# A new written-out order of operations, and the last output tile in two column halves, in a fused attention and FFN kernel

## The chip, the cores and the metric

The kernel runs on 1 core of one Trainium2 chip. The metric is the device time of one execution in microseconds (us). The time before is 236.06, the median of 3 runs (235.92 to 236.71).

## The reference, cut to what matters

```python
# q, k, v: (B=8, H=8, S=576, D=64); pool = 8, so Sp = 72 pooled keys
k_p = k.reshape(B, H, Sp, 8, D).mean(axis=3)
v_p = v.reshape(B, H, Sp, 8, D).mean(axis=3)
attn = softmax(q @ k_p.T / sqrt(D))            # 576 x 72 a head
x = (attn @ v_p), heads side by side            # (B, 576, 512)
h = relu(x @ w_in)                              # (B, 576, 1024)
conv = sum over 3 taps of conv_w[tap] * h shifted by tap - 1 along the sequence
out = (h * sigmoid(conv)) @ w_out               # (B, 576, 512), float32
```

## The kernel before, in words

Eight sequences are worked on in four groups of two. A group has nine tiles of up to 128 rows: tiles 0 to 3 hold rows of its first sequence, tile 4 holds 64 rows of both, tiles 5 to 8 hold rows of the second one.

**Loads.** Every input comes through the DMA queue that POOL (GpSimd) issues to: k, q and v of each sequence, w_in in two halves, w_out. They turn float32 into bf16 on the way. POOL also builds the pool matrix (L299, affine selects), the head mask (L320) and the identity. Buffers are reused: one for raw k, four for q, three for v, so later loads wait until an earlier user is done.

**Attention of a tile.** K is pooled by TensorE (PE) with the pool matrix for sequences 0 and 1 (`prep_k`, L374 and L384), and on DVE for the others (`pool_pair` L406, then a turn by PE, L412). V is pooled on DVE (`prep_v`, L434, L438, with the widened head mask of L337). q is turned by PE (`prep_q`, L464 in the form of 18 matmuls a half, L468 in the form of 36) and copied out of PSUM (L474). Then come scores (PE, L503 or L516), the maximum (DVE, L529), the shift (PE L549 in group 0, DVE L541 later), exp (ACT, L567), the turn of the exponentials (PE and a copy in groups 0 and 1, a DMA transpose on the SP queue in groups 2 and 3), values (PE, L603), the division (DVE, L616 and L618), and the turn of the result into xT (PE and a copy, or a DMA transpose).

**FFN of a sequence.** `ffn_in` (L648; for sequence 0 tile by tile, L669, in both kernels) multiplies by w_in into PSUM, ACT applies relu (L657, L679), `ffn_conv` (L730) does the convolution as matmuls with diagonal 64x64 matrices, ACT takes tanh (L741), DVE gates (L752, L755, L759), `ffn_out` (L764) multiplies by w_out, DVE or ACT copies the tile out of PSUM (L775), and SP stores it (L787), as two DMAs of 64 rows.

**What sets the order.** The program is made as a graph of some 970 operations (`add`). `Graph.order` (L138) then emits them in the sequence that the table `ORDER` gives: entry n stands for operation n // 2, its last bit chooses between the engines that it may run on, and -1 is a fill matmul, a product of zeros that occupies PE. Each engine works through its own instructions in that sequence. `FORMS` chooses between two ways of writing `prep_k`, `prep_q` and the scores. `PLACES` gives the PSUM banks, of which there are 8. The SBUF buffers of a ring (rings such as `osb`, `tg`, `e`, `x`) are taken in turn.

**The last tile** (group 3, tile 8) is accumulated in one PSUM bank by 8 matmuls of 512 columns. Its left 256 columns are copied by DVE, its right 256 by ACT; when both are done, SP stores the first 64 rows and ACT's queue the other 64 (L1098).

Of the kernel before, what the change touches and what calls it, by code (L numbers as in the profile page):

```python
# [33 lines left out]
class Graph:  # L34
# [75 lines left out]
    )  # L110
    FORMS = (
        0, 0, 1, 1, 0, 1, 1, 1, 0, 0, 0, 0, 0, 1, 1, 0, 1, 0, 0, 0, 0, 0, 0, 0, 0, 1, 0, 0, 0, 1, 0, 1, 0, 1, 1, 1, 1, 1, 1, 1,
        0, 0, 0, 0, 0, 0, 0, 0, 1, 0, 1, 0,
    )
    PLACES = (
# [8 lines left out]
    )  # L124

# [34 lines left out]
def kernel(  # L160
# [38 lines left out]
    def bank(token):  # L199
        return psum[:, token.slots[0], :]  # L200
# [956 lines left out]
```

## Time and profile before

| what | us |
|---|---|
| median of 3 runs | 236.06 (235.92 to 236.71) |
| the profiled execution | 237.85 |
| its span, first to last instruction | 235.6 |
| mean granted TensorE clock | 0.981 |
| DVE busy / ACT busy / POOL busy | 173.9 / 146.3 / 28.0 |
| first real matmul (K of sequence 0) | 6.98 |
| PE without a stop from | 151.83 |

In the profile PE is matmuls, PEld weight loads, DVE VectorE, ACT ScalarE, POOL GpSimd, SP SyncE; L764 is line 764 of the kernel before, as printed above. An x with a number counts instructions, and `<-` names what ended a wait. PEclk is the granted share of TensorE's clock. Matmuls overlap each other in the records, so a busy PE is not PE at its peak: the pace of a group is read from where it follows itself without a gap, as in the chain of work, in which 4 matmuls of 512 columns take 0.86 us and 4 of 288 columns 0.49.

### The profile page before, as it was taken

To read this page: it belongs to the slowest core of one execution; us is meant where nothing else is said; L and a number is where in the kernel's file an instruction comes from. 1 tells how busy PE (TensorE), PEld (TensorE's weight loads), DVE (VectorE), ACT (ScalarE), POOL (GpSimd) and SP (SyncE) were. 2 spreads that over 40 slices of the span, in tenths; PEclk is the share of its full clock that TensorE was granted. 3 is DMA by queue.
4 is the path that set the end of the run, shared out by engine and by line. 5 is a ranking of instruction groups with operands and counts; after the bars stand their busy time and mean duration, and the time that the engine had idled before them with its cause. 6 is when DMAs were issued, how large, how long until landed. Compare 5 with 4: busy or idle time off the path is not lost. (4 is left out here: it accounts for less than half of the span.)

```text
span 235.6 us, 7790 instructions
## 1 busy us (share of the span) xinstructions
PE 216.2 (92%) x3362; PEld 150.8 (64%) x3362; DVE 173.9 (74%) x365; ACT 146.3 (62%) x246; POOL 28.0 (12%) x45
## 2 busy tenths in 40 slices
PE   6697899969999899988998899899999999999991
PEld 2455799756678777556764477568766665875440
DVE  4489886996999999988799779769757625716510
ACT  2245668896888997749766576358434563685320
POOL 7930731110000520300000000000000000000000
PEclk9979999997999999999999999999999999999998
DMA  5999999999940299999135777656665642601596
GB/s 88 163 186 207 207 207 207 207 207 206 191 98 3 19 199 185 230 179 171 25 70 32 155 150 137 130 124 132 91 133 116 130 85 46 136 3 38 112 203 143
DMA packets 44006, 31.51 MB, mean 134 GB/s; under 512 B 23596, under 2 KB 39364, under 8 KB 43972
## 3 DMA queue, kind: packets, MB, share of 16 engines
q0 software_dynamic: 16288, 16.26, 42.9%
q1 hardware_dynamic: 27604, 14.64, 32.3%
q8 instruction: 26, 0.43, 0.8%
q10 hardware_dynamic: 80, 0.13, 0.1%
q14 instruction: 8, 0.07, 0.1%
HBM read 32.52 MB, written 9.44 MB: 178 GB/s over the span
## 5 line engine op out<-in xcount | busy, mean ns | idle before, releaser
L764 PE MATMUL psum<-w_out_sb,gT 128*128 128x512 bf16 x288 | 70.2, 382 | 0.0
L648 PE MATMUL psum<-xT,w_in_sb 128*128 128x288 bf16 x448 | 63.7, 286 | 2.3 <-ACT tg L741 2.3
L648 PEld LDWEIGHTS <-w_in_sb 128*128 128x128 bf16 x448 | 42.0, 98 | 16.5 <-issue 2.8
L657 ACT ACTIVATE hT<-psum 128x576 bf16<-128x576 f32 x56 | 35.0, 649 | 23.8 <-PE psum L648 23.6
L741 ACT ACTIVATE tg<-psum 128x576 bf16<-128x576 f32 x64 | 37.5, 652 | 12.5 <-PE psum L730 11.0
L764 PEld LDWEIGHTS <-gT 128*128 128x128 bf16 x288 | 27.0, 98 | 25.4 <-issue 0.7
L529 DVE TENSOR_REDUCE negm<-psum 128x8 f32<-128x576 f32 (+1 forms) x36 | 27.1, 752 | 5.8 <-PE psum L516 3.9
L730 PE MATMUL psum<-hT,dw 64*64 64x288 bf16 (+4 forms) x1152 | 30.3, 246 | 1.1 <-ACT eT L592 0.3
L730 PEld LDWEIGHTS <-dw 64*64 64x64 bf16 x1152 | 25.3, 107 | 8.0 <-issue 7.3
L618 DVE TENSOR_TENSOR x<-psum,r 128x512 bf16<-128x512 f32 x36 | 24.9, 692 | 1.2
L775 ACT COPY osb<-psum 128x512 f32<-128x512 f32 (+1 forms) x26 | 14.6, 581 | 16.9 <-PE psum L764 15.1
L759 DVE TENSOR_TENSOR gT<-gT,hT 128x1152 bf16<-128x1152 bf16 x32 | 24.3, 758 | 1.1
L567 ACT ACTIVATE e<-sd 128x576 bf16<-128x576 f32 x27 | 18.2, 684 | 7.9 <-DVE sd L541 4.9
L775 DVE COPY osb<-psum 128x512 f32<-128x512 f32 (+1 forms) x11 | 7.3, 667 | 19.9 <-PE psum L764 14.5
L541 DVE TENSOR_TENSOR sd<-psum,negm 128x576 f32<-128x576 f32 x27 | 20.4, 755 | 0.8
L755 DVE TENSOR_SCALAR gT<-tg 64x576 bf16<-64x576 bf16 x64 | 19.7, 309 | 1.5 <-ACT tg L741 0.2
L603 PE MATMUL psum<-vm,eT 128*128 128x130 bf16 (+5 forms) x240 | 18.4, 222 | 1.4 <-DVE negm L529 1.4
L752 DVE TENSOR_SCALAR gT<-tg 128x576 bf16<-128x576 bf16 x32 | 9.5, 305 | 11.7 <-ACT tg L741 11.6
L603 PEld LDWEIGHTS <-eT 128*128 128x128 bf16 (+1 forms) x240 | 14.5, 100 | 4.3 <-DMA eT<-e 1.5
L434 DVE TENSOR_TENSOR v<-v 128x1280 bf16<-128x1280 bf16 (+2 forms) x24 | 13.0, 542 | 0.2
L592 ACT COPY eT<-psum 128x640 bf16<-128x640 bf16 x15 | 10.3, 691 | 4.4 <-PE psum L578 4.1
L616 DVE RECIPROCAL r<-psum 128x8 f32<-128x8 f32 x36 | 7.3, 202 | 7.8 <-PE psum L603 7.6
(73 smaller groups left out, 205.9 us busy)
## 6 DMA issues: line engine op xcount, KB each, us to landing
out_dram<-osb SPq DMA_DIRECT2D x71, 128.0 KB, 2.4
v<-in_v_dram POOLq DMA_DIRECT2D x8, 512.0 KB, 18.5
qp<-in_q_dram POOLq DMA_DIRECT2D x7, 576.0 KB, 14.0
kk<-in_k_dram POOLq DMA_DIRECT2D x3, 1152.0 KB, 13.9
w_in_sb<-in_moe_w_in_dram POOLq DMA_DIRECT2D x2, 512.0 KB, 17.0
w_out_sb<-in_moe_w_out_dram POOLq DMA_DIRECT2D x1, 1024.0 KB, 20.0
kk<-in_k_dram POOLq DMA_DIRECT2D x2, 288.0 KB, 4.5
kk<-in_k_dram POOLq DMA_DIRECT2D x1, 576.0 KB, 12.8
```

The costliest lines, as they stand in the source:

```text
L529: nc.vector.tensor_reduce(out=a["m"][0:rows], in_=a["s"][0:rows, :, 0:2 * KW].rearrange("p a (h s) -> p a h s", s=Sp), axis=AX.X, op=OP.ma ...
L541: nc.vector.tensor_tensor(out=a["d"][0:rows], in0=a["s"][0:rows, :, 0:2 * KW].rearrange("p a (h s) -> p a h s", s=Sp), in1=a["m"][0:rows]. ...
L603: nc.tensor.matmul(out=a["o"][lo:hi, h // 4, (h % 4) * (D + 1):(h % 4 + x1 - x0) * (D + 1)], lhsT=a["eT"][:, j, lo:hi], rhs=buf("vm", b)[: ...
L618: nc.vector.tensor_tensor(out=a["x"][0:rows].rearrange("p (a h d) -> p a h d", a=2, d=D), in0=ov[:, :, :, 0:D], in1=r[0:rows].unsqueeze(3) ...
L648: nc.tensor.matmul(out=banks(ps)[:, j, 0:SC], lhsT=w_in_block(dc, fb), rhs=buf("xT", g)[:, dc, i * S + j * SC:i * S + (j + 1) * SC], start ...
L657: nc.scalar.activation(out=buf("hT", b)[:, fb, :].rearrange("p (a s) -> p a s", a=2), in_=banks(ps)[:, :, 0:SC], func=ACT.Relu, scale=0.5,)
L730: nc.tensor.matmul(out=banks(pss[r ^ c])[c * D:(c + 1) * D, j, lo:hi], lhsT=dw[r * D:(r + 1) * D, tap * n_fb + fb, :], rhs=hT[r * D:(r + 1 ...
L741: nc.scalar.activation(out=tg.rearrange("p (a s) -> p a s", a=2), in_=banks(ps)[:, :, 0:SC], func=ACT.Tanh, scale=0.5,)
L755: nc.vector.tensor_scalar(out=gate[r * D:(r + 1) * D, fb], in0=tg[(1 - r) * D:(2 - r) * D], scalar1=1.0, scalar2=None, op0=OP.add)
L759: nc.vector.tensor_tensor(out=gate[:, both], in0=gate[:, both], in1=buf("hT", b)[:, both], op=OP.mult)
L764: nc.tensor.matmul(out=bank(ps)[0:rows, :], lhsT=buf("gT", g)[:, fb, t * P:t * P + rows], rhs=w_out_sb[:, fb, :], start=(fb == 0), stop=(f ...
L775: copy(out=osb[0:rows, columns], in_=bank(ps)[0:rows, columns])
```

## The change

The three tables are replaced. The new `ORDER` has 21 fill matmuls where there were 25. By the engines that it chooses, ACT makes 29 output copies and DVE 8 (26 and 11 before, the last tile's halves counted each), DVE makes 4 copies of turned exponentials (3) and 2 of K of sequence 0 (1). By the new `FORMS`, 12 turns of q take the form of 18 matmuls and 6 that of 36 (9 and 9 before, without sequence 0's first ones, which are shorter); of the scores of the 36 tiles 23 take the form of 4 matmuls, 2 that of 8, and 11 that of 16 (26, 1 and 9). `PLACES` now gives the buffer of every ring, so SBUF buffers are no longer taken in turn.

At the start, POOL issued or did before: k 0 (two parts), identity, pool matrix, q 0 (two parts), q 1, v 0, k 1, head mask, q 2, w_in (two halves), v 1, k of group 1, q 3, w_out, q 4. Now: k 0 (two parts), first part of q 0, head mask, second part of q 0, pool matrix, identity, v 0, q 1, k 1, q 2, w_in (two halves), v 1, q 3, k of group 1, q 4, w_out. On PE, 17 fills, K of sequence 0, q's first part and the turn of the convolution weights become 11 fills, the turn of the convolution weights, K, q's first part, 5 fills. On DVE, the clearing of the v and kT buffers and the widened mask stand ahead of the copies of K.

The last tile is made in two column halves: 8 matmuls of 256 columns for each, each in a PSUM bank of its own, each copied by one engine and stored by two DMAs of 64 rows and 256 columns. The matmuls of tile 6 of the group stand partly between the halves. All the rest of the graph is the same; some planned durations in it, which the written-out order doesn't read, change too.

```diff
-    ORDER = (18, 4, 2, 0, 26, 8, 10, 16, 12, 30, -1, -1, -1, ...)
+    ORDER = (18, 24, 4, 6, 2, 8, 10, -1, 14, -1, 36, -1, 28, ...)
...
             for k in o.uses:
-                if k.slots is None and k.ring == "ps":
+                if k.slots is None:
                     i = next(places)
                     k.slots = list(range(i, i + k.n))
-                elif k.slots is None:
-                    i = taken[k.ring] = taken.get(k.ring, -1) + 1
-                    k.slots = [i % self.rings[k.ring]]
...
+    def half_columns(x):
+        return slice(x * d_model // 2, (x + 1) * d_model // 2)
+
-    def ffn_out(g, t, j, ps):
+    def ffn_out(g, t, fbs, ps, columns=slice(0, d_model)):
         rows = rows_of(g, t)
-        for fb in range(n_fb // 2 * j, n_fb // 2 * (j + 1)):
+        for fb in fbs:
             nc.tensor.matmul(
-                out=bank(ps)[0:rows, :],
+                out=bank(ps)[0:rows, columns],
                 lhsT=buf("gT", g)[:, fb, t * P:t * P + rows],
-                rhs=w_out_sb[:, fb, :],
+                rhs=w_out_sb[:, fb, columns],
...
-    def ffn_store(g, t, queue, only=None):
+    def ffn_store(g, t, queue, only=None, columns=slice(0, d_model)):
...
-                    out=out[b].rearrange("(p c) d -> c p d", c=C)[c],
-                    in_=osb[j * TB:(j + 1) * TB, :],
+                    out=out[b].rearrange("(p c) d -> c p d", c=C)[c, :, columns],
+                    in_=osb[j * TB:(j + 1) * TB, columns],
...
+            if b == B - 1 and n == len(n_outs[b]) - 1:
+                o = None
+                for x in range(2):
+                    sm = token("ps")
+                    o = add(pe(*[P * 2] * 8), key + x, lambda t=t, x=x, sm=sm: ffn_out(g, t, range(n_fb), sm, half_columns(x)),
+                            after=need + [wout, o], uses=[sm, gtok[g]], mode=FULL, count=16)
+                    c = add(either(0.42, 0.38), key + x, None, after=[o], uses=[osb, sm])
+                    c.emit = lambda c=c, t=t, x=x, sm=sm: ffn_copy(g, t, sm, copier(c), half_columns(x))
+                    for r, (e, queue) in enumerate((("SP", nc.sync), ("ACT" if x else "SP", nc.scalar if x else nc.sync))):
+                        add({e: 0.59}, key + x, lambda t=t, x=x, r=r, queue=queue: ffn_store(g, t, queue, r, half_columns(x)),
+                            after=[c], uses=[osb], land=(2.0, 0, 1))
+                continue
...
-            if b == B - 1 and n == len(n_outs[b]) - 1:
-                o = [add(d, key, lambda t=t, sm=sm, x=x, copy=copy: ffn_copy(g, t, sm, copy, slice(x * P * 2, (x + 1) * P * 2)),
-                         after=[o], uses=[osb, sm])
-                     for x, (d, copy) in enumerate(((dve(0.4), nc.vector.tensor_copy), (act(0.4), nc.scalar.copy)))]
-                for x, (e, queue) in enumerate((("SP", nc.sync), ("ACT", nc.scalar))):
-                    add({e: 0.59}, key, lambda t=t, x=x, queue=queue: ffn_store(g, t, queue, x), after=o, uses=[osb], land=(2.0, 0, 1))
-                continue
```

More of the change, by code (lines that the diff above doesn't have):

```diff
@@ L59 @@
     ORDER = (
[50 rows of a table removed]
[50 rows of a table added]
     )
     FORMS = (
-        0, 0, 1, 1, 0, 1, 1, 1, 0, 0, 0, 0, 0, 1, 1, 0, 1, 0, 0, 0, 0, 0, 0, 0, 0, 1, 0, 0, 0, 1, 0, 1, 0, 1, 1, 1, 1, 1, 1, 1,
-        0, 0, 0, 0, 0, 0, 0, 0, 1, 0, 1, 0,
+        1, 1, 1, 0, 0, 0, 1, 1, 0, 0, 0, 0, 0, 0, 0, 0, 0, 0, 0, 0, 0, 0, 0, 0, 0, 1, 0, 0, 0, 1, 0, 1, 0, 1, 1, 1, 1, 0, 1, 1,
+        1, 0, 0, 0, 0, 0, 0, 1, 0, 1, 1, 1,
     )
     PLACES = (
[8 rows of a table removed]
[18 rows of a table added]
     )
@@ L138, in order @@
     def order(self):
-        forms, places, spares, taken, done, seen = iter(self.FORMS), iter(self.PLACES), list(self.spares), {}, [], set()
+        forms, places, spares, done, seen = iter(self.FORMS), iter(self.PLACES), list(self.spares), [], set()
         for n in self.ORDER:
@@ L819 @@
     START = -2 * SLOTS
-    LATE = 2.0
+    LATE = 1.8
     RATE, RATE_FIRST = 400e3, 285e3
@@ L867 @@
         graph.spares.append(Op({"PE": 0.216}, 0, lambda t=t: fill(t), [t], FULL, None, 2))
-    c1 = add({"DVE": 0.6}, soon(), clear_pool_matrix)
+    c1 = add({"DVE": 1.5}, soon(), clear_pool_matrix)
     p0 = add({"POOL": 1.6}, first("pm"), build_pool_matrix, after=[c1])
@@ L874 @@
     cwtok = token("ps")
-    cwp = add({"PE": 0.1}, soon(), lambda: turn_conv_weights(cwtok), after=[idf, cwl], uses=[cwtok])
-    zv = add({"DVE": 0.55}, soon(), lambda: clear(*[v0[TB:P, 4, :] for v0 in buffers["v"]]))
+    cwp = add({"PE": 0.1}, soon(), lambda: turn_conv_weights(cwtok), after=[idf, cwl], uses=[cwtok], count=2)
+    zv = add({"DVE": 0.84}, soon(), lambda: clear(*[v0[TB:P, 4, :] for v0 in buffers["v"]]))
     ze = add({"DVE": 0.25}, soon(), lambda: clear(*[e[:, 4 * KW:] for e in buffers["e"]]))
-    zk = add({"DVE": 0.8}, soon(), lambda: clear(*buffers["kT"][1:]))
+    zk = add({"DVE": 1.25}, soon(), lambda: clear(*buffers["kT"][1:]))
     p1 = add({"DVE": 0.35}, soon(), double_pool_matrix, after=[p0])
@@ L884 @@
     hmw = add(dve(1.15), soon(), widen_mask, after=[hm])
-    dw0 = add({"DVE": 0.2}, soon(), lambda: build_conv_matrices(0, cwtok), after=[cwp], uses=[cwtok])
+    dw0 = add({"DVE": 0.3}, soon(), lambda: build_conv_matrices(0, cwtok), after=[cwp], uses=[cwtok])
     dwo = [add({"DVE": 1.0}, START + Graph.DW + n, lambda n=n: build_conv_matrices(n), after=[dw0]) for n in (1, 2)]
@@ L891, in add_load_pair @@
         loads["kk", g] = add({"POOL": 0.65}, key, lambda: load_pair(g), uses=[kk[g]], land=(LATE, 2 * kb, RATE))
-    picked = add({"DVE": 0.5}, START + Graph.DW - 1, build_pick, after=[c0])
+    picked = add({"DVE": 0.95}, START + Graph.DW - 1, build_pick, after=[c0])
     for b in (1, 2, 3):
@@ L1015, in add_att @@
         if turn_by_dma(g, t):
-            o = add({"SP": 1.29}, key, lambda: att_send(g, t), after=[o, ze], uses=[e, eT], land=(1.7, 0, 1))
+            o = add({"SP": 1.29}, key, lambda: att_send(g, t), after=[o, ze], uses=[e, eT], land=(2.1, 0, 1))
         else:
@@ L1027, in add_att @@
         if b0 >= Graph.X_DMA:
-            o = add({"SP": 1.29}, key, lambda: att_out(g, t), after=[o], uses=[x, xtok[g]], land=(1.7, 0, 1))
+            o = add({"SP": 1.29}, key, lambda: att_out(g, t), after=[o], uses=[x, xtok[g]], land=(2.1, 0, 1))
         else:
@@ L1071, in add_ffn @@
             conv = add({"PE": 0.75}, w + 6 * f2 + Graph.QCONV + nudge("c", 4 * b + f2), lambda f2=f2, cbs=cbs: ffn_conv(b, f2, cbs),
-                       after=relu[fbs[0]] + relu[fbs[1]] + dwo, uses=cbs + tgs + [htok[b], gtok[g]], mode=QUARTER, count=64 + 12 * i)
+                       after=relu[fbs[0]] + relu[fbs[1]] + dwo, uses=cbs + tgs + [htok[b], gtok[g]], mode=QUARTER, count=64 + 16 * i)
             for fb, cb, tg in zip(fbs, cbs, tgs):
@@ L1086, in add_out @@
             key += nudge("ot", 9 * g + t)
-            sm, osb = token("ps"), token("osb", g, t)
+            osb = token("osb", g, t)
+            need = [a for x in groups[g][0:i + 1] for a in gdone[x]]
+            if b == B - 1 and n == len(n_outs[b]) - 1:
[10 more added lines that the diff above has]
+                continue
+            sm = token("ps")
             o = None
             for j in range(2):
-                need = [a for x in groups[g][0:i + 1] for a in gdone[x]]
-                o = add(pe(*[512] * 4), key, lambda t=t, j=j, sm=sm: ffn_out(g, t, j, sm), after=need + [wout, o],
+                o = add(pe(*[512] * 4), key, lambda t=t, j=j, sm=sm: ffn_out(g, t, range(4 * j, 4 * j + 4), sm), after=need + [wout, o],
                         uses=[sm, gtok[g]], mode=FULL if rows == P else HALF, count=8)
-            if b == B - 1 and n == len(n_outs[b]) - 1:
-                o = [add(d, key, lambda t=t, sm=sm, x=x, copy=copy: ffn_copy(g, t, sm, copy, slice(x * P * 2, (x + 1) * P * 2)),
-                         after=[o], uses=[osb, sm])
-                     for x, (d, copy) in enumerate(((dve(0.4), nc.vector.tensor_copy), (act(0.4), nc.scalar.copy)))]
-                for x, (e, queue) in enumerate((("SP", nc.sync), ("ACT", nc.scalar))):
-                    add({e: 0.59}, key, lambda t=t, x=x, queue=queue: ffn_store(g, t, queue, x), after=o, uses=[osb], land=(2.0, 0, 1))
-                continue
             o = add(either(0.69, 0.585), key, None, after=[o], uses=[osb, sm])
```

126 rows, old and new, of tables (ORDER, PLACES) are left out of this document.

## The prediction

> **What bounds the kernel now.** First the page: busy time, the 40 slices.
>
> ```profile
> PE 216.2 (92%) x3362; PEld 150.8 (64%) x3362; DVE 173.9 (74%) x365; ACT 146.3 (62%) x246; POOL 28.0 (12%) x45
> ...
> PEclk9979999997999999999999999999999999999998
> DMA  5999999999940299999135777656665642601596
> ```
>
> PE's 92% is a mean over unlike stages, its clock dips twice, and the DMA engines are full only up to about 64 us. So the second view is the table by stretches (us; then busy PE, PEld, DVE, ACT, POOL; granted clock, DMA share, GB/s), cut where the stages change.
>
> ```profile
> 6.98:24.00 17.02, 13.22 (x304) 9.15 (x304) 13.47 (x33) 8.04 (x16) 6.66 (x12) 0.90 1.22 193
> 24.00:52.40 28.40, 25.05 (x564) 21.59 (x563) 24.21 (x53) 21.54 (x35) 9.16 (x12) 1.00 1.23 207
> 52.40:64.00 11.60, 11.60 (x108) 7.83 (x103) 9.18 (x15) 8.91 (x14) 0.00 (x0) 0.85 1.23 205
> 64.00:122.00 58.00, 54.97 (x1020) 41.76 (x1017) 54.31 (x112) 46.43 (x81) 6.46 (x9) 1.00 0.72 117
> 122.00:151.90 29.90, 27.36 (x383) 17.91 (x382) 25.21 (x45) 18.14 (x30) 0.00 (x0) 1.00 0.69 123
> 151.90:230.90 79.00, 78.87 (x984) 50.65 (x983) 44.73 (x98) 41.33 (x71) 0.00 (x0) 1.00 0.51 105
> ```
>
> From 151.9 on PE never stops, so a reordering there gains nothing but the tail. From 64 to 122 PE and DVE are both near full (54.97 and 54.31 of 58): each makes the other wait. Up to 64 the loads run at 207 GB/s without a break, and PE and DVE both have holes. Third, the chain that ended last. It is nothing but PE from 151.83, then two copies one after the other:
>
> ```profile
> 151.83 0.04 issue
> ...
> 216.91 13.93 PE psum L764 x64
> ...
> 230.92 0.44 DVE osb L775
> ...
> 231.38 0.37 ACT osb L775
> ```
>
> Fourth, the timeline of the start and the landings of single loads:
>
> ```profile
> 6.98 1.32 PE L374 MATMUL psum<-pm,kk 128*64 128x144 bf16 x36
> 18.98 1.70 DVE L434 TENSOR_TENSOR v<-v 128x1280 bf16<-128x1280 bf16 x3
> 21.43 0.87 PE L603 MATMUL psum<-vm,eT 128*128 128x130 bf16 x12
> 29.74 1.05 PE L669 MATMUL psum<-xT,w_in_sb 128*128 128x128 bf16 x16
> ```
> ```profile
> v<-in_v_dram POOLq DMA_DIRECT2D x1, 64.0 KB, 10.6
> ```
> ```profile
> w_in_sb<-in_moe_w_in_dram POOLq DMA_DIRECT2D x1, 512.0 KB, 17.9
> ```
>
> The last part of V of sequence 0 is issued at 7.95 and lands 10.6 us later, at 18.6; DVE pools it at 18.98, and the first values matmul runs at 21.43. The second half of w_in is issued at 11.52 and lands at 29.4; the first matmuls that need it run at 29.74. Both are waits for data.
>
> **The sum is made against** the profiled execution: 237.85 us, of which the span is 235.6 and 2.25 lie around it. The median of the runs is 236.06, 1.79 lower; I take the difference found on the span off that median. A measurement here tells about 0.3% (0.7 us) from no change.
>
> **Start, POOL and PE.** In the new order POOL issues from 1.31: K 1.55 (to 2.86), first part of q 0.77 (3.63), head mask 0.79 (4.42), second part of q 0.75 (5.17), pool-matrix selects 1.63 (6.80), identity 0.6 (7.4), then V. PE's first real work is now the turn of the convolution weights, behind ACT's copy of the identity (0.30, to 7.75); with its 0.3 the K matmuls start at 8.1, where they started at 6.98: **1.1 late**. q is no longer late (it was issued at 4.98 and landed 4.4 later, at 9.4; now issued at 2.86, behind K in the same queue). K 1.2, q 0.5, five fill matmuls 1.1: first scores near 11.1 against 10.34, 0.8 late.
>
> **Start, DVE.** Between the first maximum (11.13) and the values at 21.43 DVE had clearing of kT 1.22, half the convolution matrices 0.89, mask_wide 1.14 and a q copy 0.75 on top of the maxima. The new order clears kT and builds mask_wide ahead of or beside the K matmuls, where DVE waited, and sets the others later. What is left there: four maxima 3.0, q copy 0.5, mask columns 0.5, V 1.70 and 0.66: 6.4 from 11.45, so 17.8, where 21.4 was: **3.5 early**, if V is there. V is issued at about 7.4, as before, but ahead of q of sequence 1 (576 KB, 2.8 us at 207 GB/s): it lands near 15 instead of 18.6.
>
> **Start, loads.** That lead can't all be kept: the FFN of sequence 0 needs w_in, behind the same bytes as before (K, q, V of 0; K, q of 1; q of 2). What moves it is the hole in the stream: after K landed at 6.9 the first 256 KB of q, worth 1.3 us at 207 GB/s, landed at 9.4, so 1.1 was idle. V took 4.5 us for 2.8 us worth of bytes, another 1.7 that may or may not go. w_in lands 1.1 to 2.8 earlier; I take **2.0**, the middle, since PE is busy 9.8 of 10 us from 30 to 40 and carries such a lead on unchanged.
>
> **44 to 64.** PE loses most here: 0.40 busy in 50 to 52, with a 1.8 us wait put down to issue, and then the clock at 0.61 and 0.53 from 52 to 56. I added, for each order, the row durations of all that stands ahead of one and the same operation. Ahead of the turn of the pooled K of group 1 stand 39.2 us of DVE work before and 37.3 after; q of sequences 3 and 4 also moves up. DVE is full there (9.7 of 10), so that is up to 1.9; I take half, **1.0**, as the work is deferred and not gone.
>
> **64 to 152.** The same sums: at the last convolution of sequence 2, PE 96.5 and DVE 111.1 before, 100.2 and 115.0 after: DVE leads by 14.6 and 14.8. At the last of sequence 4: 11.4 and 12.3. In between it is worse: at the last values of group 1, 9.9 (t 100.6) and 12.1. A larger lead of DVE work means that PE waits longer: 0.2 to 2.2 lost, nearest to the two later points, **0.4**.
>
> **Forms and fills.** Four fills fewer (0.22 each, -0.9); three q turns take the 18-matmul form (0.63) for the 36-matmul form (0.33): +0.9. Scores change form within 0.1. Copies: DVE has three output copies fewer (0.69 each) and two others more (0.48, 0.31), ACT the reverse: inside the DVE sums above. Nothing net.
>
> **Tail.** The last tile was 8 matmuls of 512 columns, then DVE 0.44 and ACT 0.37 in series (one bank), then a store on SP and one on ACT at 231.78, landing 2.3 and 2.6 later. Now 16 matmuls of 256 columns: the same columns, 8 more starts, which no row here shows; bounds from the nearest rows: 0 (w_in matmuls of 288 columns follow at 0.12 each, without a gap for weights) to 8 x 0.1 (a weight load, mean 98 ns, if none were hidden); I take 0. The second half has its own bank, one copy of 0.42, saving 0.4. But on SP its store stands behind four others: two of the first half, two of tile 6, whose copy ends 0.2 before PE does; they take 0.6 each, so the last store is issued 1.15 after PE's end, where it was 0.9. ACT's lands earlier, SP's at 1.15 + 2.3 = 3.45 after PE's end; it was 3.5. **0.1 gained**, with bounds of -0.5 and +0.8.
>
> **Sum:** -2.0 - 1.0 + 0.4 - 0.1 = -2.7: span 232.9, profiled 235.15, median **233.3**.
>
> **A rule and the rows.** The clock fell to half for about 3.4 us twice: 0.83 over 10 to 20 and over 50 to 60, after stretches in which PE was at work about half the time (0.90 of 2 in 8 to 10, 0.40 of 2 in 50 to 52), with no single wait over 1.9. The Trainium skill (TensorE: Matmul & The Clock Gate, Part 1) has the clock halve after an idle window of about 3.4 us. By that rule neither dip should be here; the trace disagrees, so short waits count, and the new start, with PE idle from about 5.9 to 7.75, can dip too.
>
> **Rivals.** (1) *More is gained:* the q and K work of the next sequences moves up, so the 1.8 us wait and the dip at 52 (3.4 us at half speed, 1.7) go altogether, with w_in 2.8 early: -2.8 - 1.8 - 1.7 = -6.3, 229.8. For it: w_out and q of sequence 4 stand early enough in the new queue. Against: the wait is put down to issue, not to data. (2) *Given back:* the lead is spent where DVE is full, 64 to 122; the 2.2 at group 1 is not recovered, so 3.0 - 2.2 - 0.1: 235.2 to 236. (3) *Slower:* one mechanism, DVE at the attention of group 1 (90 to 104). The order asks 2.2 us more DVE work there ahead of PE's, PE has no other ready work, and the waits bring a third dip of the clock (1.7), while w_in comes no earlier because V and q share its queue as before (0.3 lead left): +3.6, 239. It decides once the lead at 64 us is under 2.2. For it: DVE is idle under 0.4 in each 10 us from 60 to 100. Against: the sums meet again by sequence 2. (4) *A dip at the start* (K and q at half speed, 1.7 more): values near 19.5, still before 21.4; it changes little. That the change doesn't do what it says isn't a case: the order of instructions is written out.
>
> **How the numbers follow.** Forecast, 231 to 235.3: 0.52. More, 228.5 to 231: 0.18. Given back, of which half within 0.3% and a little on the fast side: 0.11. Slower, 236.8 to 240: 0.19. Faster 0.73 (0.52, 0.18 and 0.03), within 0.3% 0.08, slower 0.19. The range leaves out about a tenth at each end: 230.0 to 238.0.
>
> **What would show it.** Right: V of sequence 0 lands near 15; the first values matmul runs before 19; w_in's second half lands at 28 or earlier; no dip near 52; PE without a stop from about 149. Wrong: w_in landing at 29 as before, or PE waiting on DVE by more than 2 us between 90 and 110. The tail: the last landing about 3.4 after PE's end.

## The result and the profile after

The changed kernel takes **240.02 us** (median of 4 runs, 237.52 to 240.78) where the kernel before took 235.99 beside it: a ratio of 1.0126, with a 95% interval of 1.008 to 1.0172. Forecast were 233.3 and a range of 230.0 to 238.0, so both the sign and the range were wrong. A second measurement was milder: 238.78 (12 runs) against 237.56, ratio 1.0035 (0.9996 to 1.0073). By this second ratio the time would be 236.9, inside the range and not told from no change. So the changed kernel is slower by something between nothing and 1.7%, and by no measurement faster. The profiled execution took 239.91 with a span of 237.8, 2.2 more than the span before. A ratio is taken from undisturbed executions alone and a median from all of them, so kernels are compared here by their ratios, and the profiles of the kernels with one move and with three moves, taken in disturbed executions, are read for places and the order of things only.

The page of the kernel after, with the same three rows:

```profile
PE 216.1 (91%) x3340; PEld 151.1 (64%) x3340; DVE 172.2 (72%) x364; ACT 146.7 (62%) x247; POOL 27.7 (12%) x45
...
PEclk9999999999999999979999999988999999999999
DMA  5999999999923999951544467776236541062696
```

A dip is a stretch in which TensorE's granted clock is at half. The two dips of before, at 12 and at 52, are gone; two new ones stand at 104 and 160. The table by stretches (us; busy PE, PEld, DVE, ACT, POOL; granted clock, DMA share, GB/s), cut as before:

```profile
6.98:24.00 17.02, 14.28 (x318) 10.47 (x319) 13.46 (x41) 9.00 (x17) 8.36 (x13) 1.00 1.24 200
24.00:52.40 28.40, 26.10 (x538) 22.19 (x536) 24.65 (x47) 23.26 (x37) 8.04 (x11) 1.00 1.24 207
52.40:64.00 11.60, 11.30 (x144) 8.49 (x142) 11.50 (x22) 10.24 (x19) 0.00 (x0) 1.00 1.23 207
64.00:122.00 58.00, 52.61 (x979) 38.59 (x978) 49.09 (x99) 41.52 (x72) 5.71 (x8) 0.97 0.73 120
122.00:151.90 29.90, 29.13 (x360) 19.77 (x360) 27.27 (x53) 17.27 (x30) 0.00 (x0) 1.00 0.58 108
151.90:230.90 79.00, 76.21 (x985) 48.68 (x984) 41.77 (x93) 43.15 (x75) 0.00 (x0) 0.98 0.49 101
```

Up to 64 PE is better off than before. The loss stands in two rows: from 64 to 122 PE is busy 52.6 where it was 55.0, and behind 151.9, where it never stopped before, 76.2 of 79. I laid both traces over each other by equal work of PE (the row durations of all real matmuls, added in order). The changed kernel leads by 3.35 us at 40, 5.7 at 64, 5.5 at 100; by 1.1 at 112, 3.2 at 154, -0.4 at 166, -1.5 at 226. These leads are an estimate, good to about 1 us, as they depend on how overlapping rows are added. So it won more than forecast and lost it at single places.

**The first place** is 99 to 104. Windows of 2 us, then the timeline of PE and of ACT there (start, length, what, times; in brackets the wait before it and what ended it):

```profile
100.00:102.00 2.00, 0.00 (x0) 0.00 (x0) 1.94 (x4) 0.00 (x0) 0.00 (x0) 1.00 1.11 214
102.00:104.00 2.00, 0.09 (x6) 0.09 (x8) 0.04 (x1) 1.22 (x3) 0.00 (x0) 1.00 1.08 158
104.00:106.00 2.00, 2.00 (x58) 1.53 (x58) 0.00 (x0) 1.75 (x4) 0.00 (x0) 0.61 0.32 59
106.00:108.00 2.00, 2.00 (x12) 1.08 (x11) 0.00 (x0) 1.18 (x3) 0.00 (x0) 0.54 0.00 0
```
```profile
98.44 1.06 PE L737 MATMUL psum<-hT,dw 64*64 64x288 bf16 x41
103.91 1.21 PE L737 MATMUL psum<-hT,dw 64*64 64x288 bf16 x39 [4.40 <-ACT osb L785]
```
```profile
102.78 1.07 ACT L785 COPY osb<-psum 128x512 f32<-128x512 f32 x2 [4.51 <-DMA out_dram<-osb]
```

PE does nothing for 4.7 us. (A stop is counted in this text from the start of one weight load of PE to the start of the next; the brackets of a row give the gap between the matmuls, which is a little shorter.) PE needs PSUM banks 6 and 7, which ACT has yet to copy out; ACT waits for the buffer `osb` 0, which still waits to be stored. Afterwards the clock is 0.61 and 0.54 for 4 us, which costs 4 less 2.3, 1.7. DVE isn't what PE waits for: it works on until 102 and then runs dry. Why a buffer that was filled at 53 is not yet stored at 102, the SP queue tells (start, time, what):

```profile
80.84 1.30 SPq L594 DMA_TRANSPOSE eT<-e  x1
82.20 2.53 SPq L797 DMA_DIRECT2D out_dram<-osb  x4
93.97 1.20 SPq L634 DMA_TRANSPOSE xT<-x  x1
95.22 2.76 SPq L797 DMA_DIRECT2D out_dram<-osb  x4
```

SP issues in order. From 84.7 to 93.97 it stands at a transpose of x (group 2, tile 3; "g2 t3" from here on) whose data are not ready: they need the values of that tile, and DVE's division. Behind it stand the stores of tiles 1 and 3 of group 0. They are issued from 95.22 on, while the last of a burst of loads still flow (k of group 3, v of 5 and 6 and q of 6, issued from 73.6 to 77.3 and landed by 96.6; v of 7, issued at 92.0 and landed at 99.9). The one that matters, of g0 t1, lands at 102.0 and 102.7, its two halves, where a store otherwise takes 2.4.

In the kernel before, SP stands even longer at a transpose of x, from 87.9 to 99.65:

```profile
83.89 1.35 SPq L587 DMA_TRANSPOSE eT<-e  x1
85.29 2.57 SPq L787 DMA_DIRECT2D out_dram<-osb  x4
99.65 1.20 SPq L627 DMA_TRANSPOSE xT<-x  x1
101.04 8.16 SPq L587 DMA_TRANSPOSE eT<-e  x3
109.30 1.17 SPq L787 DMA_DIRECT2D out_dram<-osb  x2
```
```profile
97.55 0.59 ACT L775 COPY osb<-psum 128x512 f32<-128x512 f32 x1 [0.58 <-PE psum L764]
```

But behind it stand three transposes and no store that a copy waits for: ACT's copy there waits for PE alone. So it isn't SP's waiting that costs, but what stands behind the entry that waits.

**The second and third place** are in the chain that ended last (start, us, what), which before held nothing but PE there:

```profile
154.37 4.27 DMA eT<-e
...
190.62 3.46 DMA out_dram<-osb
```

At 154.37 SP sends the exponentials of g3 t0, ready since 151.6 but behind four stores and a transpose of x; PE waits for them and stops for 2.45, and the clock falls again (0.76, 0.50 and 0.89 in 158 to 164, another 1.7). At 190.6 the second half of the store of g1 t0, copied 33 us earlier, goes out behind transposes and other stores; ACT waits for its buffer, and PE stops for 1.0.

Sum: 4.7 + 1.7 + 2.45 + 1.7 + 1.0 = 11.6, less two stops of before that are gone (2.0 at 105, 1.6 at 128.6): 7.9 lost of a lead of 5.7. To that come 1.05 of PE work more (193.5 by the same rows, 192.5 before), and the stretch from the start of the last copy to the end of the span is 0.35 shorter (4.35, 4.70 before): 2.9 by this sum, where the spans differ by 2.2.

### The profile page after: what moved, and what is told of

Its sections match the earlier page's. It is cut to its first block, busy times and chain, and to the rows that moved or that the text cites. A ratio compares the mean times of both kernels' runs of the same rounds, so it can differ in the third digit from the quotient of the medians.

```text
span 237.8 us, 7761 instructions
## 1 busy us (share of the span) xinstructions
PE 216.1 (91%) x3340; PEld 151.1 (64%) x3340; DVE 172.2 (72%) x364; ACT 146.7 (62%) x247; POOL 27.7 (12%) x45
## 4 chain that ended last, share of the span: by engine, by line
PE 44%; DVE 4%; DMA 3%; issue 2%; ACT 1%; SPq 1%; ACTq 0%; DVEq 0%
PE psum L774 21%; PE psum L655 14%; PE psum L737 5%; PE psum L610 2%; DMA eT<-e 2%; DMA out_dram<-osb 1%; DVE gT L762 1%; PE psum L523 1%; ACT tg L748 1%; DVE gT L766 1%; DVE qT L481 1%; SPq L797 1%; PE psum L475 0%; DVE gT L759 0%; PE psum L510 0%
## 5 line engine op out<-in xcount | busy, mean ns | idle before, releaser
L774 PE MATMUL psum<-w_out_sb,gT 128*128 128x512 bf16 (+1 forms) x296 | 71.4, 382 | 0.2
L774 PEld LDWEIGHTS <-gT 128*128 128x128 bf16 x296 | 27.9, 99 | 26.4 <-issue 2.1
L785 ACT COPY osb<-psum 128x512 f32<-128x512 f32 (+1 forms) x29 | 16.6, 579 | 30.6 <-PE psum L774 19.9
L610 PE MATMUL psum<-vm,eT 128*128 128x130 bf16 (+5 forms) x240 | 18.9, 224 | 4.1 <-DMA eT<-e 2.3
L785 DVE COPY osb<-psum 128x512 f32<-128x512 f32 (+1 forms) x8 | 5.2, 656 | 14.7 <-PE psum L774 14.7
L481 ACT COPY qT<-psum 128x1152 bf16<-128x1152 bf16 (+2 forms) x11 | 10.8, 985 | 4.2 <-PE psum L471 4.1
```

Source lines behind the costliest of these rows:

```text
L610: nc.tensor.matmul(out=a["o"][lo:hi, h // 4, (h % 4) * (D + 1):(h % 4 + x1 - x0) * (D + 1)], lhsT=a["eT"][:, j, lo:hi], rhs=buf("vm", b)[: ...
L774: nc.tensor.matmul(out=bank(ps)[0:rows, columns], lhsT=buf("gT", g)[:, fb, t * P:t * P + rows], rhs=w_out_sb[:, fb, columns], start=(fb == 0),
L785: copy(out=osb[0:rows, columns], in_=bank(ps)[0:rows, columns])
```

## The experiments

Moves change the emitted list of operations alone, not the buffers or banks: with a list of pairs, element n of the list is put right behind another one. PE's own instructions stay in their order.

```diff
+        at = list(done)
+        for n, behind in MOVES:
+            done.remove(at[n])
+            done.insert(done.index(at[behind]) + 1, at[n])
```

**The tail alone.** The kernel before with its own order, and only the last tile in two halves.

```diff
-    ORDER, FORMS, PLACES = (those of the change)
+    ORDER, FORMS, PLACES = (those of before, with the last tile's new operations at the end)
```

> The order, the forms and the banks of the kernel before; only the last tile is made in two column halves, with banks, copies and stores of their own. The forecast's tail term: 0.1 us gained, with bounds of 0.5 gained and 0.8 lost, so 235.2 to 236.8 against 236.0. If instead the tail is what made the changed kernel slower, it comes out near 240.

Measured: 236.81 against 236.46, ratio 1.0014 (0.9983 to 1.0045). In its profile the last landing is 234.30 - 230.55 = 3.75 after DVE starts its last copy (at 230.55); with the old tail it was 3.49 (234.41 - 230.92). The halves neither gain nor lose anything to be measured, to about 0.4%. What is left of the change is the three tables; forms and buffers were not tried apart from the order.

**One move on SP: the stores ahead of the waiting transpose.** The transpose of x of g2 t3 is put behind the stores of g0 t1 and t3.

```diff
+        MOVES = [(454, 467)]
```

> The changed kernel with one move on SP's queue: the transpose of x of tile 3 of group 2, which waits there until 93.97, goes behind the two stores that follow it. Theory SP (stores that are ready stand behind a waiting transpose, an output buffer is not given back, ACT's copy waits 4.5 us, and PE with it): the stores are issued near 85 to 86, the PE wait of 5 us at 99 to 104 goes, and the half-clock stretch behind it (1.7 us); 233 to 235.5. Theory Loads (the burst of loads from 73.6 on delays every landing by some 10 us, whatever stands where): the stall only moves, 239 or more. Theory Order (PE and DVE work in a poorer order, the queue is a symptom): 239 to 240.

Measured: 235.42, ratio 0.9945 (0.9907 to 0.9984). The stores now go out from 84.7 on, and one operation that costs SP the same either way turns the loss into a small gain. The stop near 99 didn't go, though: it became another one, in which PE waits for nothing that the profile shows. PE's timeline:

```profile
98.06 1.33 PE L745 MATMUL psum<-hT,dw 64*64 64x288 bf16 x49
102.02 1.31 PE L745 MATMUL psum<-hT,dw 64*64 64x63 bf16 x31 [2.63 <-issue]
```

49 of 80 matmuls run, which is one convolution of 40 and 9 of the next, although the first four matmuls of a convolution already write all four of its banks and read both of its inputs. What ends near there is a fetch of PE's own instructions: the queue that the page of the profile calls instruction moved 16 KB from 98.11 on, and took 2.55 (2.53 at the same place in the changed kernel) where the shorter ones take 0.9. It makes 26 such fetches in a run, one for every 257 or 258 of the 6695 instructions recorded for PE.

**Fewer loads.** v of sequences 5 to 7 brings only its last 64 rows, q of sequence 6 only one of four pairs of heads; the rest of those buffers holds older data, so the output is not the reference's.

```diff
+        if b == 6:
+            part = {"heads": slice(0, 1)}
...
+        if b < 5:
             nc.gpsimd.dma_start(
                 out=vt[:, 0:4, :], in_=rows[0:4 * P].rearrange("(j p) x -> p j x", p=P)
```

> The changed kernel without most of four loads: of V of sequences 5, 6 and 7 only the last 64 rows are loaded, of q of sequence 6 one pair of heads of four; the output of these sequences is another one. Theory Loads, and theory SP too in so far as the burst is what makes the transposes late: the transpose of the exponentials issued near 81 lands in 3 to 4 us where it took 11.3, the PE wait at 99 goes, 233 to 235.5. If SP's order alone matters, and not the landings: the wait stays, 239 or more.

Measured: 234.16, ratio 0.9875 (0.9816 to 0.9933). The transpose sent at 80.75 now lands at 85.72, not 92. Still SP issues the transpose of x only at 93.88 and the stores at 95.12: late landing was not what held SP, its place in the order was. What the loads did is to stretch the store from there: both halves have landed 3.7 later here, 7.5 in the changed kernel. The stop shrinks to 1.07 and its dip goes. The stops at 156 (2.8 here) and 194 (1.2) stay, only sooner, as there are no loads near them in either kernel.

**Three moves on SP.** The move above; the transpose of the exponentials of g3 t0 earlier and the store of g1 t8 later; the store of g1 t0 earlier.

```diff
+        MOVES = [(454, 467), (691, 709), (703, 694), (841, 803)]
```

> As the one move before, and two more on SP: the transpose of the exponentials of tile 0 of group 3 right behind its exp, ahead of a store and of a transpose of x; the store of tile 0 of group 1, which is issued at 190 though its tile was copied some 35 us earlier, moved up by five operations of that queue. Theory SP: the waits at 99 (5.0), 156 (2.0) and 193 (0.9) go, and two half-clock stretches (1.7 each): 229 to 232. Theory Loads: only the waits at 156 and 193 go, 236 to 238. Theory Order: 239 to 240.

Measured: 233.47, ratio 0.9853 (0.9799 to 0.9908): faster than both kernels, though not as far as theory SP had it (229 to 232). The stop at 193 is gone; one is left near 100, where PE waits for nothing that the profile shows, and one near 160, where ACT's copy waits for a store.

**The changed kernel again.**

> The changed kernel itself once more, beside the kernels below on the same chip. Both theories expect the first measurement again: 240, at least 1% above the kernel before, with the stop of TensorE near 99 to 104 in its profile.

Measured: 238.78, ratio 1.0035 (0.9996 to 1.0073). The stops are there at the same places (3.3 at 99.5, 2.7 at 155, 1.3 at 193), the store landing at 101.6. Not the 1% that was expected: by how much the order loses isn't fixed to better than that between the two measurements.

**The late moves alone.**

```diff
+        MOVES = [(691, 709), (703, 694), (841, 803)]
```

> The changed kernel with only the two late moves on SyncE's queue: the transpose of g3 t0 and the store beside it ahead of where they stood (the stop of 2.4 at 156), and the store of g1 t0 ahead of the transposes it stood behind (the stop of 1.0 at 194). The stop at 99 to 104 is left alone. Theory queue order: the two stops and the dip after the first go, 2.4 + 1.0 + about 0.6 of clock, so 3 to 4 less than the changed kernel: 236 to 237. Theory load burst (all of the loss arises while loads fill the DMA engines, 77 to 97): nothing changes by more than 1, 239 to 240.

Measured: 236.13, ratio 0.9922 (0.9886 to 0.9957), by the ratios 2.7 under the changed kernel beside it. The stop at 99 stays (3.2, with its dip); that for the exponentials at 156 and that at 194 are gone, and one of 1.15 without a dip is left at 158, where ACT's copy waits for a store. So the loss doesn't all arise under the loads.

**A load moved into a hole.** From 68 to 74 the DMA engines are idle, and POOL waits until 73.6 for the buffer of k. q of sequence 6, whose buffer is free, goes ahead of that wait.

```diff
+        MOVES = [(400, 334)]
```

> The changed kernel with the load of q of sequence 6 moved on GpSimd ahead of the load that waits until 73.6 for its buffer; its own buffer has been free since about 50. It then runs from 68 to 73, where the DMA engines moved 0 to 8 GB/s, and 1.18 MB (5.7 at 207 GB/s) go from the burst, which ends near 91 instead of 97. Nothing on SyncE moves. Theory load burst: the transpose sent at 80.8 lands 4 to 6 sooner, what stands behind it too, and the stop of 4.7 at 99 and its dip (1.5) go: 4 to 6 less, 234 to 236. Theory queue order alone: the stop shrinks by less than 2, 238 to 239. A third reading, from the traces of the last runs: behind that stop lies another, in which TensorE waits for its own instructions (a fetch of 16 KB that took 2.5 instead of 0.95 while the loads ran, with TensorE stopped in the middle of a convolution at one and the same place of its stream in two kernels). If that is right, the fetch near 98 takes about 0.95 here and no such stop is left.

Measured: 236.07, ratio 0.9962 (0.9931 to 0.9993), by the ratios 1.7 under the changed kernel beside it, less than the load theory's 4 to 6. The expectation had a mistake: 207 GB/s counts bytes as written, 576 KB, so the load is worth 2.8 and not 5.7. And the transpose lands at 90.65, only 1.2 sooner than in the run beside it: v of 5 and 6 were issued ahead of it still, and it lands about when v of 6 does (its two parts at 91.2 and 91.9). The store lands at 100.5 instead of 101.6, the stop is 2.4 instead of 3.3, and the fetch of instructions takes 0.89.

**All four.**

```diff
+        MOVES = [(454, 467), (691, 709), (703, 694), (841, 803), (400, 334)]
```

> The changed kernel with the three moves on SyncE and the early load of q of sequence 6 together. If both theories hold and their parts are separate: the stops at 99, 156 and 194 all go, and so does the wait of TensorE for instructions near 100; against the kernel with the three moves alone 1.5 to 3 less, 231 to 232. If the load burst costs nothing once the stores are out of the way: the same as with the three moves, 233.5.

Measured: **232.63**, ratio 0.9829 (0.9784 to 0.9874), the fastest of all; span 229.7. That the early load adds to the three moves isn't shown (the intervals overlap). Its clock row has no dip:

```profile
PEclk9999999999999999999999999999999999999999
```

A stop is left at 99.1, again after the 9th matmul of the same convolution (the pause of PE's weight loads is 1.30), and one of 1.6 at 154.6, where ACT's copy waits 2.5 for a store.

```profile
98.08 1.33 PE L745 MATMUL psum<-hT,dw 64*64 64x288 bf16 x49
100.42 0.76 PE L745 MATMUL psum<-hT,dw 64*64 64x63 bf16 x31 [1.01 <-issue]
```

**All four again**, on another chip.

> The kernel with the four moves once more, as the base for the three beside it on the same chip: 232.6 again, ratio to the kernel before 0.979 to 0.987.

Measured: 232.35 against 236.3, ratio 0.983 (0.9794 to 0.9866).

**What the stop at 99 waits for.** Two turns of q, which run at 35 and 46, take the form with twice the matmuls.

```diff
-        1, 1, 1, 0, 0, 0, 1, 1, 0, 0, 0, 0, 0, 0, 0, 0, 0, ...
+        1, 1, 1, 0, 0, 0, 1, 1, 0, 0, 0, 0, 0, 0, 1, 0, 1, ...
```

> The four moves, and the two turns of q of sequence 3 (near 30 and 45) in the form of 36 matmuls instead of 18: 36 more matmuls and 36 more weight loads in TensorE's stream ahead of the stop at 99, which comes in the middle of the convolution (b 3, fourth pair of blocks), after its 9th matmul. Theory instructions (TensorE has run into the end of what it has fetched): the stop comes at the same place of the stream, 36 matmuls earlier in the work: after about the 13th matmul of the convolution ahead of it. Rival, data (a bank or a buffer that the 10th matmul waits for): it stays after the 9th matmul of the same convolution. The time says little: 232 to 233.

Measured: 233.49, ratio 0.9868 (0.9821 to 0.9915). Neither theory's place: the stop is gone. PE's timeline:

```profile
98.86 1.80 PE L745 MATMUL psum<-hT,dw 64*64 64x288 bf16 x80
```

Both convolutions run through, with the same data, banks and buffers as before. That speaks against the rival: what changed is the stream of instructions 50 to 65 us earlier. The fetch that began at 97.5 in the kernel with four moves begins at 94.2 here. Counting PE's recorded instructions from the start (weight loads, matmuls and the few that wait for semaphores), the stop lay at instruction 3266; pauses of 1.0 and 0.7 now stand at 1473 and 1730, the first in the middle of a convolution:

```profile
44.00 0.31 PE L745 MATMUL psum<-hT,dw 64*64 64x63 bf16 x3 [0.64 <-issue]
```

These numbers leave 194, 193 and 194 when divided by 256, the instructions of 64 bytes that 16 KB hold. So does 1729 (193), where the *kernel before* stopped at 49.88, between the second and the third of four matmuls of one turn:

```profile
49.88 0.28 PE L635 MATMUL psum<-ident,x 128*128 128x128 bf16 x2
51.76 0.29 PE L635 MATMUL psum<-ident,x 128*128 128x128 bf16 x2 [1.60 <-issue]
```

There a fetch ended at 50.33, 1.4 before PE went on; in the kernels with one, three and four moves it ended 1.4, 1.5 and 1.5 before, and at the two pauses of this kernel 1.4 and 1.5. So PE ran into the end of the instructions that it had. In the kernel before, the fetches that begin while loads flow (up to 55.4, and from 90.0 to 103.9) begin 2.2 to 3.9 us after PE has entered a block, each for the block behind it, and all others 1.4 us after that or sooner. So PE stops where it works through its 256 instructions in less than this wait, the fetch and the 1.4 together: the block that ended in the stop at 49.88 was entered at 45.83, the fetch began at 49.43 and took 0.89. Why a fetch begins later under loads isn't shown. The Trainium skill (Runtime: NRT & Kernel Launch, Instruction fetch mechanics) says that instructions come in blocks of 16 KiB, 256 of them, and that crossing a boundary is mostly hidden. The trace agrees: of the 26 fetches in the kernel with four moves one ends in a stop of over 0.6 us, and that one took 1.3.

**Without the first move.**

```diff
+        MOVES = [(691, 709), (703, 694), (841, 803), (400, 334)]
```

> The four moves without the first one: the stores of g0 t1 and t3 stand on SyncE behind the transpose of x of g2 t3 again. If that transpose is what made the stop at 99, the stop comes back as in the kernel with q of sequence 6 early alone (2.4 instead of 1.3), with a dip of the clock in most executions (1.7 more): 234 to 236. If the late moves and the load had mended it already: 232.6, as with all four.

Measured: 235.61, ratio 0.9881 (0.9829 to 0.9933) beside 0.983: 1.2 us more by the ratios, whose intervals overlap, so the size isn't settled. In the trace the stop is back (2.6, ACT's copy waiting 2.5 for the store, and the dip). So the place of this one transpose on SP makes the stop by itself, also with the rest mended.

**A store left in place.**

```diff
+        MOVES = [(454, 467), (703, 694), (841, 803), (400, 334)]
```

> The four moves, but in the second of them only the transpose of g3 t0 is sent sooner, and the stores of g1 t8 stay ahead of it, where the change had put them. With the four moves TensorE still stops 1.6 at 154.6, because ScalarE's copy waits 2.5 for that store. Theory queue order: the store lands some 3 sooner, the transpose 1 to 2 later than with the four moves but sooner than in the changed kernel; the stop shrinks below 1: 231 to 232. If the transpose is again the later of the two: a stop of 1 to 2 that waits for it, 232.6 to 233.

Measured: 233.65 beside 232.35, ratio 0.9882 (0.9832 to 0.9932). The expectation failed: the stop at 154.4 grew to 2.6, with a dip behind it. ACT's copy of g1 t0 doesn't wait for the stores of g1 t8 but for that of g1 t3, the next in the order, which now went out at 153.90 instead of 153.17. Moving that one wasn't tried.

## Why the prediction was wrong

**Right.** *Start, POOL and PE*: K at 7.88 (8.1 forecast), first scores at 10.96 (11.1). *Start, DVE*: first values at 17.85 (17.8). The dip at the start, rival (4), did not come. *Tail*: the last landing is 236.89, 3.4 after the last copy starts (3.45 after PE's end was forecast), and the tail alone measures as no change.

**Right in sign, and too small.** *Start, loads* had 2.0: v of sequence 0 landed at 13.8 instead of near 15, and the lead at 40 was 3.35. But w_in landed at 28.3, only 1.1 earlier than before (28 or earlier was forecast), and the matmuls that need it run at 28.37 instead of 29.74. So only 1.4 of the lead is the wait for w_in that the term had; the rest is other work that PE had done by then. *44 to 64* had 1.0 and brought 2.35, since PE's stop at 50 and its dip went altogether, as rival (1) had it. That stop was put down to issue, and I read this as a sign that nothing could be gained there; it was the end of a block of instructions, whose place moves with any change of the stream.

**Wrong: *64 to 152*, 0.4 lost, and "from 151.9 on PE never stops, so a reordering there gains nothing but the tail".** Both were worked out from two sums, of PE's work and of DVE's, as if these two alone could make each other wait. SP's queue was not in it. In the new order SP takes stores behind transposes that wait for their data, stores hold `osb`, `osb` holds ACT's copies, and these hold the banks that PE needs next. That cost 4.7 at 99 and 1.0 at 194; at 156 it is the other way round, a transpose that is ready stands behind four stores and another transpose, PE waits for it, and it cost 2.45. To that come 3.4 of clock behind the first and the second stop. A reordering where PE never stops can gain nothing, but it can lose, and the second sentence left that out. The sign "PE without a stop from about 149" failed with it. Rival (3) had the place, 90 to 104, a dip there and the time, by luck: its mechanism was another (PE waited for a store and not for DVE), the lead at 64 was 5.7, far above the 2.2 under which it was to decide, and its own sum of +3.6 gives 239.7, not 239.

**Wrong by 1: *forms and fills*, nothing net.** The 0.9 for the three longer turns of q (among sequences 1 to 7, 8 turns take the form of 18 matmuls and 6 that of 36, where 5 and 9 did before) is work on the path; the 0.9 of the four fills stood in PE's idle time at the start and was no gain to set against it. PE's work without fills is 1.05 more by the rows, and this 1 us is the term that had been put at nothing.

**The rule.** By the Trainium skill (TensorE: Matmul & The Clock Gate, Part 1) an idle window of about 3.4 us is what halves the clock. The stop of 4.7 agrees with that, being longer. The dips after 2.45 (changed kernel) and 2.4 (early load) don't, and a stop of 2.3 at 154 in that last kernel had none. So the length of the wait alone doesn't decide here. The price of a dip is the same in each of these profiles, 3.4 us at half speed, 1.7.

## What to carry to other kernels

Where one engine's queue carries both stores and transposes that wait for data, read it as a third order beside those of the engines: for each instruction that waits, list what stands behind it, how old its data are, and which buffer it holds. A ready store behind one waiting transpose cost more here (3.3 and 4.7 in two profiles, and a dip each time) than the 0.2 to 2.2 that the prediction weighed between PE's and DVE's work, and moving SP's entries alone turned a loss of 0.3 to 1.3% into a gain of 1.5%. A queue that waits costs nothing by itself: in the kernel before SP stood 11.8 us at a transpose, and no copy waited for what was behind it. A wait taken away can show another behind it: look at what would have been late next before counting its whole length.

## What the runs showed of the hardware

- TensorE stops in the middle of an operation, "issue" in the profile, at places one or more blocks of 256 instructions apart, when a fetch of 16 KB ends late: it goes on 1.4 to 1.7 us after the end of that fetch, in the kernels of this text. The stop was 1.9 us near 50 in the kernel before and 1.3 near 99 in the one with four moves, both while loads filled the DMA engines.
- A transpose sent while loads of some 14 us (2.9 MB at 207 GB/s, an estimate) are under way lands late: from 80.8 to 92.2 in the changed kernel, beside the load of v of 6 that was issued 4.9 us ahead of it and landed at 92.6; from 80.75 to 85.7 with most of these bytes left out. A store took 7.5 instead of 2.4 at the end of that stretch.
- The granted clock differs between executions of one kernel: its mean went from 0.978 to 1.000 over the runs of the kernel before, from 0.979 to 0.993 over those of the changed one, and from 0.995 to 1.000 over those of the one with four moves. A dip of 3.4 us at half speed is 0.7% of the span, so this is the size of up to three dips (an estimate). The times of the kernel before spread over more than 1%, not over the 0.3% that the prediction took.
